# Weight forms split once, split tiles loaded three times, and a new order of the attention part, in a kernel of attention, linear memory and two MLPs

## The chip, the cores and the metric

The kernel runs on one core of one Trainium2 chip. The core has a matrix engine (TensorE, PE in the profile, with its weight load PEld beside it), VectorE (DVE), ScalarE (ACT), GpSimd (POOL) and a DMA queue that SyncE (SP) and ScalarE can issue to. Each engine runs its own list of instructions in order and waits on semaphores for the others. The metric is the device time of one execution in microseconds (us), the median over runs.

## The reference

q, k and v have 4 batches, 8 heads, 576 tokens and 64 columns. Each head's output is a gated mix of causal softmax attention and of a linear memory that is given (`M_prev`, `z_prev`). The 2304 x 512 result goes through two MLPs in float32; the weights arrive in float64.

```python
scores = where(causal, -1e9, q @ k.T / sqrt(D))
local  = (softmax(scores)) @ v
mem    = (phi(q) @ M_prev) / (phi(q) . z_prev + 1e-6)      # phi = elu + 1
x = g * mem + (1 - g) * local                              # g = sigmoid(beta) per head
h = x @ w_in;  r = maximum(h, 0)                           # 2304 x 2048
y = (s * r * r + b) @ w_out                                # 2304 x 512, s and b scalars
gate = sigmoid(y @ w_gate);  val = y @ w_val               # 2304 x 1536 each
out = (gate * val) @ w_out2                                # 2304 x 512
```

## The kernel before

Nearly every product is made of float32 values split in a high part (a cast to the PE's rounded format, written fp32r) and a low part (the value less its high part): high by high, low by high, high by low, three matmuls for one. The split is a cast on ACT and a subtraction on DVE or POOL.

The stages follow each other on PE. Attention runs in jobs of two heads: q and k come as raw tokens, are transposed on PE (`qt`, `kt`, L443), split, multiplied to scores (`sc`), put through the exponential, transposed (`pt`) and multiplied with v (`o`); the memory's products are `ret`. The jobs in `DIRECT` are written by `prep_direct` (its tiles at L964 to L1031), the others by `plan_prep`. Finished windows of x feed `h` (L321), whose rectified blocks go to DRAM (`relu_scratch`) and come back in `y`.

In `y` a step is one window of 384 tokens by 128 rows of r. `plan_step` loads it (`rr`, six buffers), squares it on ACT (L1446), makes s r^2 + b on POOL (`scale`, L1450), casts it (`gh`, L1456), subtracts (`gl` on DVE, L1461) and multiplies (L1475, 12 matmuls). After 16 steps `plan_y_out` brings the sums of a window out of PSUM (`evict`) and, but for the first two windows, stores them (`y_scratch`). During `y`, `plan_blocks` takes the float64 blocks of w_gate and w_val to float32 and makes seven forms of each group of weights (two copies and four sums and differences, `wm`), 12 groups, stored as plain float32 in `weight_scratch`.

The third stage takes the windows in three pairs. `plan_t` makes seven combinations of the two windows' y, split. `plan_group` (12 groups in a pair) loads a group's forms (`wf`, L1683, 896 KB), splits them (cast L1688 on ACT, subtraction L1696, one of four on DVE and three on POOL by `LOS`), multiplies the seven forms with the seven combinations (`m`, L1712, 42 matmuls), and adds the results up (`plus`, L1724 on DVE; sigmoid L1728 on ACT; the product of gate and value, `times`, L1734 on POOL). `plan_out` splits these products (`ps`, L1792 and L1805) and multiplies them with w_out2 (`o`, L1815, 216 matmuls in a pair). In the first pair the 12 tiles of w_out2 are brought from float64 too: three steps on DVE (L255, L258, L264), a cast (L270) and a subtraction on POOL (L273), in `weight_parts`.

What sets the order is a planner, the class `Plan`: every task is added with its engine, a cost in ns, an urgency made from the table `TUNE`, what it reads and writes, and which numbered buffers (`slots`) it takes. `order` plays the tasks against these costs and writes each engine's list. `RING` is the number of split tiles `ws`, `PACE` says after which steps of `y` a group's forms may be made.

Of the kernel before, what the change touches and what calls it, by code (L numbers as in the profile page):

```python
# [20 lines left out]
FB = 1  # L21
# [10 lines left out]
}  # L32
ENG = {"split": "DVE", "join": "POOL"}
# [4 lines left out]
RING = 5  # L38
SETS = 3
PACE = 2, 7  # L40


class Plan:
# [6 lines left out]
    def add(self, eng, ns, fn, urgency, reads=(), writes=(), new=(), late=60, size=0):  # L50
# [15 lines left out]
        self.tasks.append([eng, ns, fn, urgency, after, used, new, late, size])  # L66
        return n

    def order(self):
# [23 lines left out]
        out, events, now, dma = [], [], 0, 0  # L93
# [10 lines left out]
        while len(out) < len(tasks):  # L104
            for eng in clock:
                if clock[eng] > now:
                    continue
                for n in ready.get(eng, []):
# [44 lines left out]
def attention_moe_kernel(  # L153
# [41 lines left out]
    wf_d = dram("weight_scratch", [NF2, P, 7 * 2 * P])  # L195
# [15 lines left out]
    sb_b = const.tile([P, 1], F32, name="sb_b")  # L211

# [260 lines left out]
    def mm(n):  # L473
        return max(108, 15 + n // 2.35)
# [1481 lines left out]
```

## Time and profile before

| What | Value |
|---|---|
| median of 3 runs | 1077.78 us (1076.87 to 1078.69) |
| the profiled execution | 1078.23 us |
| its span in the trace | 1076.4 us |
| PE busy | 1043.2 us, 97% of the span, 6696 matmuls |
| DVE, ACT, POOL busy | 69%, 58%, 52% |
| DMA | 145.56 MB, mean 135 GB/s |

The span is the stretch between the first and the last instruction recorded; busy time is the sum over an engine's instructions with overlaps counted once. By the chain of waits (the work that ended last, followed back from the end) `h`, `m`, `y` and `o` of the third stage are the largest pieces. In the order of time the attention part fills about the first 80 us, then attention and `h` run mixed to about 400, `y` reaches to 646, the first pair to 797, the second to 935.

### The profile page before, as it was taken

Reading aid. Unit: us, or ns where it says so; the run is one execution under the profiler, and the core shown is the slowest. Engines: PE = TensorE matmul, PEld = TensorE weight load, DVE = VectorE, ACT = ScalarE, POOL = GpSimd, SP = SyncE. Lnnn points to the kernel's source line nnn. Section 1 sums busy time; section 2 is a strip of 40 time slices with the busy share of each in tenths; the row PEclk is TensorE's granted clock in tenths of the full one; section 3 lists DMA queues with packets and bytes.
Section 4 is the critical chain, followed back from the end, with each engine's and each line's share of the span. In section 5 each row is a group of like instructions: output and inputs, shape, how many; then the busy total and the mean of one; then the engine's idle time right before and its main releaser. Section 6 shows DMA issues by size and latency. Waiting matters only on the chain.

```text
span 1076.4 us, 19037 instructions
## 1 busy us (share of the span) xinstructions
PE 1043.2 (97%) x6696; PEld 981.2 (91%) x6696; DVE 741.1 (69%) x1408; ACT 623.8 (58%) x1341; POOL 560.9 (52%) x546
## 2 busy tenths in 40 slices
PE   6998999999999999999999999998999999999998
PEld 5887998899999999999999999887889998899986
DVE  4777887766776647557988747999736676266631
ACT  4766878767777656556667646554335453354431
POOL 1336466354344417535966537987428773277600
PEclk9998999999999999999999999999999999999999
DMA  5434453233332148657499766543223430133101
GB/s 136 108 78 124 141 162 102 73 100 92 88 88 69 50 142 271 205 180 251 149 332 299 258 246 219 182 162 108 88 79 123 138 104 30 64 137 109 63 20 40
DMA packets 135023, 145.56 MB, mean 135 GB/s; under 512 B 68112, under 2 KB 122896, under 8 KB 134928
## 3 DMA queue, kind: packets, MB, share of 16 engines
q1 hardware_dynamic: 134496, 144.35, 42.2%
q8 instruction: 53, 0.87, 0.3%
q14 instruction: 42, 0.34, 0.1%
q10 hardware_dynamic: 432, 0.01, 0.0%
HBM read 106.57 MB, written 37.75 MB: 134 GB/s over the span
## 4 chain that ended last, share of the span: by engine, by line
PE 82%; DVE 8%; POOL 4%; ACT 2%; DMA 2%; issue 2%; SPq 0%; DVEq 0%; ACTq 0%; POOLq 0%
PE h L321 18%; PE m L1712 18%; PE y L1475 17%; PE o L1815 14%; PE sc L673 3%; DVE set L1724 2%; PE o L1212 2%; PE acc L854 1%; PE acc L853 1%; PE pt_B L800 1%; DVE raw_w_out L258 1%; POOL rr L1450 1%; PE kt L443 1%; PE acc L857 1%; PE sc L699 1%
## 5 line engine op out<-in xcount | busy, mean ns | idle before, releaser
L1712 PE MATMUL m<-yt,ws 128*128 128x384 f32 x1512 | 265.2, 335 | 3.7 <-DVE set L1724 3.2
L1712 PEld LDWEIGHTS m<-yt,ws 128*128 128x128 f32 x1512 | 261.9, 188 | 6.8 <-DVE set L1724 4.9
L321 PE MATMUL h<-x,w_in 128*128 128x256 f32 (+1 forms) x1536 | 228.9, 301 | 1.9 <-DVE x L942 1.6
L321 PEld LDWEIGHTS h<-x,w_in 128*128 128x128 f32 x1536 | 210.0, 190 | 8.3 <-issue 3.2
L1724 DVE TENSOR_TENSOR set<-m,set 128x384 f32<-128x384 f32 x252 | 134.5, 554 | 58.7 <-PE m L1712 55.4
L1696 POOL TENSOR_TENSOR ws<-wf,ws 128x512 fp32r<-128x512 f32 (+1 forms) x108 | 124.3, 1171 | 83.5 <-ACT ws L1688 83.5
L1450 POOL TENSOR_SCALAR rr<-rr,sb_s,sb_b 128x384 f32<-128x384 f32 x96 | 111.6, 1170 | 99.6 <-ACT rr L1446 87.0
L1815 PE MATMUL o<-w_out,ps 128*128 128x512 f32 x648 | 154.5, 400 | 4.4 <-DVE ps L1805 4.2
L1815 PEld LDWEIGHTS o<-w_out,ps 128*128 128x128 f32 x648 | 123.5, 191 | 34.7 <-DVE ps L1805 4.5
L1475 PE MATMUL y<-gh,w_out 128*128 128x384 f32 x768 | 149.3, 335 | 1.1 <-POOL w_out L273 0.6
L1475 PEld LDWEIGHTS y<-gh,w_out 128*128 128x128 f32 x768 | 133.9, 188 | 2.1 <-POOL w_out L273 0.9
L1688 ACT CAST ws<-wf 128x512 fp32r<-128x512 f32 (+1 forms) x144 | 81.0, 567 | 88.1 <-PE m L1712 63.1
L1461 DVE TENSOR_TENSOR gl<-rr,gh 128x384 fp32r<-128x384 f32 x96 | 69.4, 728 | 56.8 <-ACT gh L1456 31.9
L1734 POOL TENSOR_TENSOR p<-set,set 128x384 f32<-128x384 f32 x72 | 84.1, 1188 | 43.1 <-DVE set L1724 43.1
L731 POOL TENSOR_SCALAR P<-P,rs 128x256 f32<-128x256 f32 (+4 forms) x108 | 62.7, 601 | 67.2 <-DVE rs L727 26.3
L653 DVE CUSTOM_DVE_ANT_0 P<-sc,mask 128x256 f32<-128x256 f32 (+4 forms) x144 | 69.9, 515 | 35.8 <-PE sc L673 13.8
L331 ACT ACTIVATE r<-h 128x320 f32<-128x320 f32 (+1 forms) x128 | 52.2, 409 | 72.6 <-PE h L321 58.5
L1475 PE MATMUL y<-gl,w_out 128*128 128x384 f32 x384 | 82.3, 335 | 0.8 <-DVE gl L1461 0.8
L1805 DVE TENSOR_TENSOR ps<-p,ps 128x512 fp32r<-128x512 f32 x54 | 49.4, 933 | 42.6 <-ACT ps L1792 42.3
L1792 ACT CAST ps<-p 128x512 fp32r<-128x512 f32 x54 | 32.5, 619 | 72.2 <-PE o L1815 60.6
L1475 PEld LDWEIGHTS y<-gl,w_out 128*128 128x128 f32 x384 | 67.8, 188 | 1.5 <-DVE gl L1461 1.5
L715 ACT ACTIVATE P<-P,nm 128x256 f32<-128x256 f32 (+4 forms) x108 | 62.9, 583 | 5.2 <-DVE nm L653 4.9
(185 smaller groups left out, 1623.8 us busy)
## 6 DMA issues: line engine op xcount, KB each, us to landing
wf<-weight_scratch SPq DMA_DIRECT2D x36, 896.0 KB, 4.6
rr<-relu_scratch SPq DMA_DIRECT2D x96, 192.0 KB, 4.0
raw_w_out<-in_moe_w_out_dram SPq DMA_DIRECT2D x28, 512.0 KB, 4.1
weight_scratch<-wm SPq DMA_DIRECT2D x12, 896.0 KB, 6.3
relu_scratch<-r SPq DMA_DIRECT2D x32, 320.0 KB, 2.4
raw_w_in<-in_moe_w_in_dram SPq DMA_DIRECT2D x16, 512.0 KB, 4.0
relu_scratch<-r SPq DMA_DIRECT2D x32, 256.0 KB, 2.8
raw_gv<-in_moe_w_gate_dram SPq DMA_DIRECT2D x12, 512.0 KB, 4.3
```

Of the source, the lines that this page charges most:

```text
L321: nc.tensor.matmul(t[:, :n], wt[:, wi, c], x[:, xi, c], start=(m == 0), stop=(m == 3 * NK - 1))
L653: nc.vector.tensor_tensor_reduce(out=pr, in0=ps, in1=mk, scale=1.0, scalar=3e38, op0=ALU.add, op1=ALU.min, accum_out=nm,)
L715: nc.scalar.activation(pr, pr, AF.Exp, bias=T.pop(("nm", j, e, t)), scale=-1.0, accum_out=T["sums", j][:, col : col + 1],)
L1450: nc.gpsimd.tensor_scalar(out=r, in0=r, scalar1=sb_s, scalar2=sb_b, op0=ALU.mult, op1=ALU.add)
L1461: nc.vector.tensor_tensor(out=gl, in0=r_sb.pop(step), in1=gs[step][0].bitcast(F32), op=ALU.subtract)
L1475: nc.tensor.matmul(accs[wi][d][:, :n], w_out_sb[f][:, x, d], y, start=(f == 0 and x == 0 and y is gh), stop=(f == NF - 1 and y is gl),)
L1688: nc.scalar.copy(t[:, 0, :m], flat(a, m))
L1696: engine[LOS[i]].tensor_tensor(out=t[:, 1, :m], in0=flat(a, m), in1=t[:, 0, :m].bitcast(F32), op=ALU.subtract)
L1712: nc.tensor.matmul(acc, wt[:, a, k : k + P], yt[:, y, c], start=(m == 0), stop=(m == 3 * K2 - 1),)
L1724: nc.vector.tensor_tensor(out=t[:, o], in0=Z["m", z, x], in1=t[:, i], op=ALU.add)
L1734: engine[TIMES[o]].tensor_tensor(out=p[:, f + HF * OF[o][0], OF[o][1]], in0=Z["set", z][:, o], in1=Z["set", zg][:, o], op=ALU.mult,)
L1815: nc.tensor.matmul(Z["zo", z], Z["ps", z, i][:, a, k * P : (k + 1) * P], w_out2_sb[f][:, x].rearrange("p c f -> p (c f)"), start=(i == k = ...
```

## The change

The matmuls of `h`, `y`, `m` and `o` stay as many as they were. Four things change.

*Forms.* `plan_blocks` splits each group's forms at once, as it makes them: `sums` makes the four sums and differences, `form` finds each pair of forms, `hi` casts it on ACT, `lo` subtracts on DVE (all four of `LOS`), `store` writes high and low part side by side. `weight_scratch` grows to four tiles of 128 x 1024 a group (the last half full). `plan_group` splits nothing; it loads the four tiles straight into `ws`, 4 loads where 1 was. `RING` goes from 5 to 7, `PACE` from (2, 7) to (0, 6).

*y.* `scale` goes; only r^2 is made. Two columns of ones beside the r of the first window give the column sums of w_out in the same matmuls (386 columns wide there, not 384), and s and b come in as y leaves PSUM.

*Pairs.* `SEQ` takes the pairs in the order 0, 2, 1: the last two windows of `y` go into the second pair as they are, so their stores and loads fall away (8 stores, 2 loads).

*Attention.* q and k have two raw buffers each, not one. The first q comes over ScalarE's queue. The memory's result (`MX`) sits in buffers of another tile. All costs of the planner and the table `TUNE` are new, and a task can hold a port that others wait for in the planner's play (`held`).

```diff
-RING = 5
+RING = 7
-PACE = 2, 7
+PACE = 0, 6
+LOS = ("DVE", "DVE", "DVE", "DVE")
-    "mem": 39.5, "lq": -622.0, "lk": -752.9, "lv": -921.7, "lm": 533.7, "q": -351.0,
+    "mem": -121814.8, "lq": 2020.0, "lk": -111329.7, "lv": 2438.5, "lm": 740.6, "q": -34627.0,
...
-    wf_d = dram("weight_scratch", [NF2, P, 7 * 2 * P])
+    wf_d = dram("weight_scratch", [NF2, 4, P, 1024])
...
-    rawq = at.tile([P, NQ, P], F32, name="rawq", bufs=1)
-    rawk = at.tile([P, NQ, P], F32, name="rawk", bufs=1)
+    rawqs = [at.tile([P, NQ, P], F32, name=f"rawq{i}", bufs=1) for i in range(2)]
+    rawks = [at.tile([P, NQ, P], F32, name=f"rawk{i}", bufs=1) for i in range(2)]
...
+        eng = nc.scalar if src is q and j == 0 else nc.sync
         for e in range(2):
-            nc.sync.dma_start(
+            eng.dma_start(
...
+    SEQ = [0, NW // 2 - 1, *range(1, NW // 2 - 1)]
...
+        def ones():
+            nc.gpsimd.memset(r_sb[step][:, n:], 1.0)
...
-        def scale():
-            r = r_sb[step]
-            nc.gpsimd.tensor_scalar(
-                out=r, in0=r, scalar1=sb_s, scalar2=sb_b, op0=ALU.mult, op1=ALU.add
-            )
...
+            if wi == 0:
+                nc.vector.tensor_scalar(
+                    out=sb_c[:, d : d + 1], in0=accs[wi][d][:, n : n + 1], scalar1=sb_b, scalar2=None,
+                    op0=ALU.mult,
+                )
...
-                nc.vector.tensor_copy(yf[wi][:, d], accs[wi][d][:, :n])
+                nc.vector.tensor_scalar(
+                    out=yf[wi][:, d], in0=accs[wi][d][:, :n], scalar1=sb_s,
+                    scalar2=sb_c[:, d : d + 1], op0=ALU.mult, op1=ALU.add,
+                )
...
-            if wi >= 2:
+            if wi // 2 not in (SEQ[0], SEQ[1]):
...
+        def hi(i):
+            box[i] = Y["ws"].tile([P, 2, 512], F32R, tag="ws", name=f"wp{n}_{i}")
+            nc.scalar.copy(half(i, 0), form(i)[0])
+
+        def lo(i):
+            engine[LOS[i]].tensor_tensor(
+                out=half(i, 1), in0=form(i)[0], in1=half(i, 0).bitcast(F32), op=ALU.subtract
+            )
+
+        def store(i):
+            m = form(i)[1] * P
+            nc.sync.dma_start(
+                wf_d[n, i, :, : 2 * m].rearrange("p (x m) -> p x m", x=2),
+                box.pop(i)[:, :, :m].bitcast(F32),
+            )
...
-        def load():
-            t = Z["wf", z] = Y["wf"].tile([P, 7, K2, P], F32, tag="wf", name=f"wf{pi}_{n}")
-            nc.sync.dma_start(t.rearrange("p a c f -> p (a c f)"), wf_d[n])
...
+        def load(i):
+            m = len(PAIRS[i]) * 2 * P
             t = Z["ws", z, i] = Y["ws"].tile([P, 2, 512], F32R, tag="ws", name=f"ws{pi}_{n}_{i}")
-            nc.scalar.copy(t[:, 0, :m], flat(a, m))
...
+            nc.sync.dma_start(
+                t[:, :, :m].bitcast(F32), wf_d[n, i, :, : 2 * m].rearrange("p (x m) -> p x m", x=2)
+            )
```

In the first pair POOL's list reads, before, at about the fourth group (`w_out_4` to `w_out_7` are tiles of w_out2, `ws` are low parts of forms, `p` products of gate and value):

```order
L273 TENSOR_TENSOR w_out_4_9015<-raw_w_out_4_9013,w_out_4_9015 128x512
L1696 TENSOR_TENSOR ws_3_3_9166<-wf_3_9027,ws_3_3_9166 128x256
L1734 TENSOR_TENSOR p_8852<-set_8_9108,set_2_9023 128x384 x3
L1696 TENSOR_TENSOR ws_9_1_9219<-wf_9_9111,ws_9_1_9219 128x512
L1696 TENSOR_TENSOR ws_9_2_9229<-wf_9_9111,ws_9_2_9229 128x512
L1734 TENSOR_TENSOR p_8852<-set_8_9108,set_2_9023 128x384
L1696 TENSOR_TENSOR ws_9_3_9254<-wf_9_9111,ws_9_3_9254 128x256
L273 TENSOR_TENSOR w_out_5_9127<-raw_w_out_5_9125,w_out_5_9127 128x512
```

After, at the same place:

```order
L278 TENSOR_TENSOR w_out_3_8921<-raw_w_out_3_8919,w_out_3_8921 128x512
L1809 TENSOR_TENSOR p_8893<-set_7_9013,set_1_8915 128x384 x4
L278 TENSOR_TENSOR w_out_4_9000<-raw_w_out_4_8998,w_out_4_9000 128x512
L278 TENSOR_TENSOR w_out_5_9057<-raw_w_out_5_9055,w_out_5_9057 128x512
L1809 TENSOR_TENSOR p_8893<-set_8_9164,set_2_9081 128x384 x4
L278 TENSOR_TENSOR w_out_6_9142<-raw_w_out_6_9140,w_out_6_9142 128x512
```

The low parts of forms are gone from it; products and tiles of w_out2 follow each other.

SP's list of loads at that place, before (`raw_w_out_7` is a tile of w_out2 in float64):

```order
L1683 DMA wf_4_9196<-weight_scratch 128x1792
L1683 DMA wf_10_9283<-weight_scratch 128x1792
L239 DMA raw_w_out_7_9294<-in_moe_w_out_dram 128x1024
L1683 DMA wf_5_9365<-weight_scratch 128x1792
L239 DMA raw_w_out_8_9379<-in_moe_w_out_dram 128x1024
```

and after:

```order
L1771 DMA ws_3_0_9113<-weight_scratch 128x1024
L1771 DMA ws_3_1_9135<-weight_scratch 128x1024
L244 DMA raw_w_out_6_9140<-in_moe_w_out_dram 128x1024
L1771 DMA ws_3_2_9152<-weight_scratch 128x1024
L1771 DMA ws_3_3_9186<-weight_scratch 128x2x256
L1771 DMA ws_9_0_9196<-weight_scratch 128x1024
L244 DMA raw_w_out_7_9200<-in_moe_w_out_dram 128x1024
```

One load of 1792 columns has become four, three of 1024 and one of 2 x 256.

At the start of the program ACT's list, with what each instruction waits for, is before:

```order
L215 DMA gt<-in_beta_dram 128x8
L216 DMA sb_s<-in_moe_s_dram 128x1
L217 DMA sb_b<-in_moe_b_dram 128x1
L218 ACT_TABLE_LOAD
L218 ACTIVATE gt<-gt 128x8 [waits DMAHW0_49]
L998 CAST KT_159<-kt_153 128x576 [waits PE_49]
L964 ACTIVATE phi_171<-qt_165 128x640 [waits PE_49]
L966 ACTIVATE QT_173<-qt_165 128x640
```

and after:

```order
L220 DMA gt<-in_beta_dram 128x8
L221 DMA sb_s<-in_moe_s_dram 128x1
L222 DMA sb_b<-in_moe_b_dram 128x1
L395 DMA rawq_91<-in_q_dram 128x4x64
L223 ACT_TABLE_LOAD
L223 ACTIVATE gt<-gt 128x8 [waits DMAHW0_49]
L395 DMA rawq_91<-in_q_dram 128x4x64 [waits DMAHW2_49]
L401 DMA rawq_91<-in_q_dram 64x64 [waits DMAHW4_49]
L401 DMA rawq_91<-in_q_dram 64x64 [waits DMAHW6_49]
L1002 ACTIVATE phi_174<-qt_165 128x640 [waits PE_49]
L1004 ACTIVATE QT_176<-qt_165 128x640
```

Four loads of q stand on ACT's queue now; DMAHW2, 4 and 6 are the semaphores of the loads of sb_s, of sb_b and of the third load of k. PE's list at the start is before:

```order
L443 MATMUL kt_153<-ident,rawk 128x128 x5
L443 MATMUL qt_165<-ident,rawq 128x128 x5
L1079 MATMUL sc_0_0_185<-KT_159,QT_173 128x128
L1079 MATMUL sc_1_0_186<-KT_159,QT_173 128x128
L1079 MATMUL sc_0_0_185<-KT_159,QT_173 128x128
```

and after:

```order
L451 MATMUL qt_165<-ident,rawq_91 128x128 x5
L1063 MATMUL ret_0_190<-mem_150,phi_174 128x65
L1063 MATMUL ret_1_191<-mem_150,phi_174 128x65
L1063 MATMUL ret_0_190<-mem_150,phi_174 128x65
L1063 MATMUL ret_1_191<-mem_150,phi_174 128x65
L1063 MATMUL ret_0_190<-mem_150,phi_174 128x65
L1063 MATMUL ret_1_191<-mem_150,phi_174 128x65
L1063 MATMUL ret_0_190<-mem_150,phi_174 128x65
L1063 MATMUL ret_1_191<-mem_150,phi_174 128x65
L1069 MATMUL ret_0_190<-mem_150,phi_174 64x65 x2
L451 MATMUL kt_206<-ident,rawk_93 128x128 x5
L451 MATMUL kt_229<-ident,rawk_94 128x128 x5
L1118 MATMUL sc_0_0_235<-KT_221,QT_176 128x128
```

The transposes of k stood first and come behind those of q and behind the ten matmuls `ret` now, those of the next job (`rawk_94`) right after, and the first scores behind both. Up to the first `h` PE's list has 425 rows before and 473 after.

## Rows read from the trace of the kernel before

**Rows 1.** The page, busy time, share of the span and instructions of each engine.

```profile
PE 1043.2 (97%) x6696; PEld 981.2 (91%) x6696; DVE 741.1 (69%) x1408; ACT 623.8 (58%) x1341; POOL 560.9 (52%) x546
```

**Rows 2.** Chain of waits, 645 to 935 us: start us, length us, what.

```profile
645.89 11.48 PE m L1712 x66
...
797.21 87.39 PE m L1712 x504
884.60 50.39 PE o L1815 x216
```

**Rows 3.** Windows: length, PE, PEld, DVE, ACT, POOL busy, clock, DMA share, GB/s.

```profile
0.00:80.00 80.00, 67.58 (x579) 57.52 (x580) 54.36 (x167) 50.10 (x96) 21.13 (x39) 0.98 0.44 107
80.00:400.00 320.00, 313.14 (x2502) 297.25 (x2501) 231.18 (x564) 231.87 (x576) 149.82 (x189) 0.99 0.35 100
400.00:550.00 150.00, 147.83 (x909) 145.57 (x908) 110.15 (x160) 93.01 (x197) 95.53 (x74) 1.00 0.69 224
475.00:650.00 175.00, 173.87 (x1000) 172.85 (x1000) 130.51 (x218) 106.24 (x224) 102.36 (x81) 1.00 0.75 249
675.00:750.00 75.00, 67.38 (x366) 63.07 (x364) 72.71 (x98) 41.63 (x80) 67.93 (x54) 0.99 0.46 155
800.00:875.00 75.00, 75.00 (x435) 75.00 (x434) 49.69 (x82) 38.69 (x73) 55.07 (x51) 1.00 0.37 124
```

**Rows 4.** Groups of lines, 646 to 746 us: busy us, mean ns | idle before.

```profile
L1724 DVE TENSOR_TENSOR set<-m,set 128x384 f32<-128x384 f32 x84 | 43.3, 551 | 6.1 <-PE m L1712 3.4 <-ACT f_w_out L252 0.7
L1696 POOL TENSOR_TENSOR ws<-wf,ws 128x512 fp32r<-128x512 f32 (+1 forms) x33 | 42.0, 1291 | 18.1 <-ACT ws L1688 18.1
L1734 POOL TENSOR_TENSOR p<-set,set 128x384 f32<-128x384 f32 x23 | 28.4, 1251 | 2.3 <-DVE set L1724 2.3
...
L258 DVE SCALAR_TENSOR_TENSOR raw_w_out<-raw_w_out 128x512 int32<-128x512 int32 x11 | 16.1, 1459 | 0.4
L273 POOL TENSOR_TENSOR w_out<-raw_w_out,w_out 128x512 fp32r<-128x512 f32 x10 | 13.8, 1378 | 4.0 <-ACT w_out L270 4.0
L264 DVE SCALAR_TENSOR_TENSOR raw_w_out<-f_w_out,raw_w_out 128x512 int32<-128x512 int32 x11 | 13.7, 1245 | 0.4
...
L1696 DVE TENSOR_TENSOR ws<-wf,ws 128x512 fp32r<-128x512 f32 x10 | 11.0, 1097 | 1.1 <-ACT ws L1688 0.9
L255 DVE TENSOR_SCALAR raw_w_out<-raw_w_out 128x512 int32<-128x512 int32 x11 | 9.8, 894 | 0.0
```

**Rows 5.** The same view for DVE, 900 to 925 us.

```profile
L1805 DVE TENSOR_TENSOR ps<-p,ps 128x512 fp32r<-128x512 f32 x10 | 6.8, 689 | 11.2 <-ACT ps L1792 11.2
```

**Rows 6.** The page, DMA issues: count, KB each, median us to landing.

```profile
wf<-weight_scratch SPq DMA_DIRECT2D x36, 896.0 KB, 4.6
rr<-relu_scratch SPq DMA_DIRECT2D x96, 192.0 KB, 4.0
...
rawq<-in_q_dram SPq DMA_DIRECT2D x32, 128.0 KB, 2.6
```

**Rows 7.** The page, GB/s in 40 equal slices of the span.

```profile
GB/s 136 108 78 124 141 162 102 73 100 92 88 88 69 50 142 271 205 180 251 149 332 299 258 246 219 182 162 108 88 79 123 138 104 30 64 137 109 63 20 40
```

**Rows 8.** The page, the costliest groups: the scale and shift in y.

```profile
L1450 POOL TENSOR_SCALAR rr<-rr,sb_s,sb_b 128x384 f32<-128x384 f32 x96 | 111.6, 1170 | 99.6 <-ACT rr L1446 87.0 <-DMA rr<-relu_scratch 6.5 <-DVE wm L1580 4.1
```

**Rows 9.** Chain of waits of the first 60 us: start us, length us, what.

```profile
1.24 4.78 DMA rawk<-in_k_dram
...
8.16 0.77 DVE KT L1002
...
8.97 1.34 PE qt L443 x5
...
11.67 0.84 DVE QT L974
...
12.55 2.40 PE sc L1079 x16
...
23.55 1.04 PE ret L1025 x16
```

More of the change, by code (lines that the diff above doesn't have):

```diff
@@ L65, in add @@
         used = set(reads) | set(writes) | {x for _, x in new}
-        self.tasks.append([eng, ns, fn, urgency, after, used, new, late, size])
+        self.tasks.append([eng, ns, fn, urgency, after, used, new, late, size, port])
         return n
@@ L742, in plan_scores @@
                 add(
-                    "PE", sum(3 * mm(keys(t)) for t in ts) + 190, lambda ts=ts: score(ts), w,
+                    "PE", sum(3 * mm(keys(t)) for t in ts) + 60, lambda ts=ts: score(ts), w,
                     reads=[("QT", j), ("KT", j)],
-                    new=[("s", ("sc", j, 0, ts[0])), ("s", ("sc", j, 1, ts[0]))], late=250,
+                    new=[("s", ("sc", j, 0, ts[0])), ("s", ("sc", j, 1, ts[0]))]
+                    + [(f"P{t}", ("P", j, e, t)) for e in range(2) for t in ts]
+                    + ([] if m else [("sums", ("sums", j))]),
+                    late=250,
                 )
@@ L1488, in plan_step @@
         )
-        add("ACT", act(n), square, v, writes=[rk])
-        add("POOL", 700, scale, v, writes=[rk])
-        add("ACT", act(n), g_hi, v, reads=[rk], new=[("gh", gk)])
-        add("DVE", 650, g_lo, v, reads=[rk, gk], new=[("gl", ("gl", step))])
+        if wi == 0:
+            add("POOL", 120, ones, v, writes=[rk])
+        add("ACT", act2(n), square, v, writes=[rk])
+        add("ACT", act2(n), g_hi, v, reads=[rk], new=[("gh", gk)])
+        add(
+            "DVE", **port(dve2(n)), fn=g_lo, urgency=v, reads=[rk, gk], new=[("gl", ("gl", step))]
+        )
         new = [("yacc", ("ya", wi))] if f == 0 else []
@@ new lines, in lo @@
+        def lo(i):
+            engine[LOS[i]].tensor_tensor(
+                out=half(i, 1), in0=form(i)[0], in1=half(i, 0).bitcast(F32), op=ALU.subtract
+            )
+        def store(i):
[3 more added lines that the diff above has]
+                box.pop(i)[:, :, :m].bitcast(F32),
+            )
+        k0, k1 = (("raw", x) for x in keys2)
+        for part in range(2):
+            add(
+                "DVE", **port(850), fn=lambda part=part: sums(part), urgency=u,
+                reads=[k0, k1, "bar2"], writes=[("wm", n)] if part else [],
+                new=[] if part else [("wf", ("wm", n))],
+            )
@@ new lines, in plan_blocks @@
+        for i, xs in enumerate(PAIRS):
+            m, k = len(xs) * 2 * P, ("wp", n, i)
+            ins = [k0, "bar2"] if i == 0 else [k1, "bar2"] if i == 3 else [("wm", n)]
+            add("ACT", act2(m), lambda i=i: hi(i), u, reads=ins, new=[("ws", k)])
+            add(
+                LOS[i], **port((dve2 if LOS[i] == "DVE" else pool2)(m)), fn=lambda i=i: lo(i),
+                urgency=u, reads=ins, writes=[k],
+            )
+            add(
+                "SP", 450, lambda i=i: store(i), u, reads=[k], writes=[("wd", n, i)], late=2500,
+                size=m * 1024,
+            )
```

282 lines of the change are left out of this document (149 added, 133 removed), and 12 rows, old and new, of the table TUNE.

## The prediction

> **What bounds the kernel now.** I read the page first: TensorE (PE) is busy 1043.2 of 1076.4 us, 97% [rows 1]. So the kernel is a queue of matmuls, and a change that leaves their number alone, as this one does, can win only what PE waits. The chain of waits gives the pace of a stage that nothing holds up: in the second pair of token windows 504 `m` matmuls took 87.39 us (173.4 ns each) and 216 `o` matmuls 50.39 us [rows 2], together 137.8. The first pair ran from 645.89 to 797.21, so 151.3 us for the same work: 13.5 us lost [rows 2]. The windows show why and where else [rows 3]: from 675 to 750 POOL is busy 67.9 of 75 us and VectorE (DVE) 72.7, and PE idles 7.6; from 800 to 875, where nothing is lost, DVE has 49.7 and POOL 55.1. In attention PE idles 12.4 us up to 80 and 6.9 from 80 to 400. From 400 to 550 it idles 2.2. All that is 13.5 + 12.4 + 6.9 + 2.2 = 35.0 us, some 3% of the time; PE's idle time counts only whole gaps, and the 67.6 busy us up to 80 hold many short matmuls that overlap, so attention has somewhat more to give than its 19.3.
>
> The profiled execution took 1078.23 us, its span 1076.4, 1.8 lie around it; it is 0.45 above the median of 1077.78. The sum is made against 1078.2.
>
> **Part 1: forms split once.** Each of three pairs now loads the weight forms as high and low parts. Before, each group split them on chip: in the first pair POOL did 33 such subtractions in the window shown at 1291 ns, 42.0 us, and DVE 10 at 1097 ns [rows 4]. All of that goes from `m`. What stays for POOL in the first pair: 24 products at 1251 ns and 12 low parts of w_out2 at 1378 ns, 30.0 + 16.5 = 46.6 us of 87.4. What stays for DVE: 84 sums at 551 ns = 46.3, and 12 tiles of w_out2 at 1459 + 1245 + 894 = 3.60 us = 43.2; together 89.5, still over 87.4. But those three durations are those of a crowded stretch. A subtraction of 128x512 took 1097 ns there, and 689 ns at 900 to 925, in the second pair's `o` stretch [rows 4, 5], where POOL has no products left to make. At 689/1097 the w_out2 tiles cost 27.1 us and DVE's sum is 73.4. So DVE lands between 73 and 90 of 87 us, and I take it nearer to the lower end, since POOL goes from full to about half: 4 of the 13.5 us stay, **9.5 are won**. The ends: all 13.5 (DVE at the quiet price), or a loss, which only the transfers can make (below).
>
> The row that carries this is the pair of durations, 1097 and 689. The Trainium skill (SBUF — State Buffer, Who interferes with whom) says that VectorE and GpSimd share one pair of ports as an exclusive lock, and that a VectorE operation with two SBUF inputs waits for all of a GpSimd operation that reads SBUF. The trace agrees in kind; by that rule each of the 36 products and low parts that POOL keeps can still hold a DVE instruction for its whole length, and DVE would end nearer 90 than 73, with a gain of 3 or 4 instead of 9.5. That is the third rival.
>
> **The transfers that this adds.** A group's load grows from 896 KB [rows 6] to twice that, three tiles of 128x1024 words and one of 128x512, 1.835 MB. In a pair that is 12 x 1.835 = 22.0 MB in 87.4 us, 252 GB/s where 124 stand now [rows 3]. The whole kernel's best slice moved 332 GB/s [rows 7], so pairs two and three stay covered with a quarter to spare: cost 0. If the cover went and the queue gave only the 249 GB/s of 475 to 650 [rows 3], a pair would take 88.4 us, 1 more each. In the first pair the 12 tiles of w_out2 come on top, each 128x1024 words, 6.3 MB: 28.3 MB in 87.4 us is 324 GB/s. At 332 that takes 85 us and is just hidden; at 249 it takes 113.7, against 100.9 now, 12.8 worse than before. I keep it within the 4 us that I left there.
>
> In `y` the stores of the forms double, 12 x 0.918 = 11.0 MB more, and 8 stores of y go, each 128x384 words, 1.6 MB. Between 475 and 650 the queue moved 249 GB/s at a share of 0.75 [rows 3], 43.6 MB; now 53.0 MB, 303 GB/s and a share of 0.91. At the three best neighbouring slices (332, 299, 258, mean 296 [rows 7]) that takes 179 us, 4 over the 175; at 332 it takes 160 and costs nothing; at 249 it would be 38 over. Behind a late load of relu(h) stand square, cast and subtraction, all in order, and PE after them; a step is 12 matmuls at the pace of `m`, 2.08 us, and six buffers cover 12.5 us against a landing of 4.0 [rows 6]. **I take 3 us lost**, between the first two ends, since the loads of weights can wait and the covered 12.5 us is far over 4.0.
>
> **Part 2: r^2 alone in y.** 96 POOL instructions of 1170 ns go, 111.6 us of POOL [rows 8], against 16 tiny fills and 4 one-column products. Most of that lies beside a busy PE. It pays where POOL was last: the idle time of 400 to 550, **2.2 us** won (ends: 0 and 2.2). DVE gets new work in `y`: per block three subtractions of 128x512 and one of half that, 3.5 x 0.689 = 2.4, so 12 x 2.4 = 29 us [rows 5], where 130.5 of 175 us are used now [rows 3]; 160 of 175 is tight but fits, and POOL's 102.4 us there shrink by most of the 96 x 1.17, which shortens DVE's own. Cost 0; if it did not shorten them, the blocks would end late and `m` start up to 5 us late.
>
> **Part 3: last tokens stay on chip; order of pairs 0, 2, 1.** Two loads and eight stores go, all hidden now; no matmul moves against its neighbours. Cost 0, ends 0 and -1.
>
> **Part 4: attention: two raw buffers and a new order.** Here the start is worse than it looks. The first four loads of q go from SP to ScalarE's queue, but the rows of the order show the last three waiting for semaphores of earlier transfers, the last of them for k's third load, which lands at 6.0 [rows 9]. A landing of 2.6 us [rows 6] after that, and q is whole at 8.6 at the earliest; its transposes start at 8.97 now [rows 9], so nothing is gained there. From then to a split q takes 3.5 us (8.97 to 12.51), so 12.1. PE's order then puts the ten memory products `ret` ahead of k's transposes: they need one more DVE pass, as long as the 0.84 of q's, and take 10/16 of 1.04: 13.6. From a whole k to a split one 2.9 us pass (6.02 to 8.93), so the first scores start at about 16.5 against 12.55 [rows 9], 4 us later. Of these a part comes back: `ret` and the next job's k are done by then, work that came later before, and DVE, which does it, is the fullest helper up to 80 with 54.4 us [rows 3]. After the start the second raw buffers let SP load a job ahead, and the order was made anew; the trace of before cannot price that. From both sides: half of the 19.3 idle us won, -9.7, or the 4 us kept whole and as much again lost to a first `h` that now stands behind 473 and not 425 other rows of PE, +8. I take the middle of the lower half: **4 us won**, since twice as many buffers give most of the idle time a way out, and the late start is paid once.
>
> **Sum.** 1078.2 - 9.5 + 3.0 - 2.2 - 4.0 = 1065.5; less 0.45 for the median: **1065 us**.
>
> **The rivals.**
> 1. *Slower: the DMA queue becomes the bound of `y` and of the first pair.* Place: 475 to 740. For it: a share of 0.91 and 324 GB/s; the 224 GB/s of 400 to 550, at 0.69, already stand beside 2.2 idle us [rows 3]. Against it: 332 GB/s was reached beside a PE that lost nothing. It decides when the queue sustains less than about 285 GB/s: at 270, `y` takes 196 us (+21), the first pair 105 (+4), and with attention's -4 and the -2.2 the time is 1078 + 19 = 1097. At 290, +8 and -3 leave 1077.
> 2. *Attention gives nothing or loses.* For it: the late q and the later `h`; attention at +8 instead of -4: 1077. Against it: the next job's k is ready earlier.
> 3. *The first pair stays tight* (DVE at the crowded price): 3.5 won instead of 9.5: 1071. For it: 89.5 of 87.4 us. Against it: POOL's share halves.
> 4. *Attention wins more:* prefetch and order take away 15 us, since the 12.4 + 6.9 idle us and the short matmuls around them both give: 1054.
> 5. *The change does not do what it says:* loads of the split forms that come late in every pair, 1 us each: 1067, inside the forecast.
>
> **How the numbers follow.** Forecast with its own range 1058 to 1071 (rivals 3 and 5 are its upper part): 0.60. Rival 4, 1044 to 1057: 0.16. Rival 2, 1072 to 1080: 0.13. Rival 1, above 1080 with the part at 1077: 0.11. A measurement of this kernel tells about 0.2%, 2.2 us: faster means below 1075.6. Faster: 0.60 + 0.16 + 0.08 of rivals 1 and 2 = 0.84. Same: 0.07. Slower: 0.09. The range of 8 in 10 leaves out a part of rival 4 below 1049 and of rival 1 above 1080.
>
> **What would show it.** First pair: the `m` and `o` stretch of 151.3 us at about 142, POOL and DVE below 9 tenths. `y`: DMA share near 0.9 from 475 to 650, and few waits on `rr`. Pairs two and three still 137.8 with 250 GB/s. First scores near 16.5 us, first `h` at 80 or later. The forecast is wrong if waits on `ws` or `rr` loads stand before PE, or if PE's idle time up to 400 differs from 15 by more than 8.

## The result, and the profile after

The changed kernel takes 1064.9 us (median of 4 runs, 1064.64 to 1066.66) against 1077.3 for the kernel before beside it (1076.62 to 1078.69): the ratio is 0.9885, interval 0.9869 to 0.9901. The forecast was 1065 us. The sum came out; four of its terms did not, and their errors cancel.

The profiled execution took 1065.1 us, its span 1063.0. The page's first part, as in [rows 1]:

```profile
PE 1037.5 (98%) x6696; PEld 979.9 (92%) x6696; DVE 696.1 (65%) x1424; ACT 564.4 (53%) x1221; POOL 315.0 (30%) x361
```

POOL lost 246 us of work and DVE 45. The chain of waits, where [rows 2] stood (start us, length us, what):

```profile
645.18 81.14 PE m L1787 x468
...
783.81 87.37 PE m L1787 x504
871.18 50.40 PE o L1884 x216
```

The first pair starts where it did (645.2 against 645.9) and ends at 783.8 instead of 797.2: 138.6 us, not 151.3. The second pair takes 137.8 as before. The windows of [rows 3] (length, PE, PEld, DVE, ACT, POOL busy, clock, DMA share, GB/s):

```profile
0.00:80.00 80.00, 63.31 (x563) 54.38 (x564) 57.11 (x173) 50.42 (x98) 23.16 (x45) 1.00 0.54 131
80.00:400.00 320.00, 316.13 (x2521) 298.42 (x2521) 226.18 (x558) 231.65 (x576) 146.67 (x187) 0.99 0.33 94
400.00:550.00 150.00, 149.47 (x917) 148.81 (x917) 118.66 (x192) 104.93 (x214) 32.55 (x35) 1.00 0.76 261
475.00:650.00 175.00, 174.35 (x994) 173.77 (x993) 139.03 (x258) 119.61 (x238) 10.69 (x5) 1.00 0.86 302
675.00:750.00 75.00, 74.42 (x405) 70.88 (x404) 59.27 (x96) 32.85 (x59) 38.03 (x31) 1.00 0.63 217
800.00:875.00 75.00, 75.00 (x429) 74.24 (x428) 43.74 (x76) 20.54 (x39) 23.62 (x23) 1.00 0.66 209
```

From 675 to 750 PE idles 0.6 us where it idled 7.6, with DVE at 59 of 75 and POOL at 38. Up to 80 it idles 16.7, more than the 12.4 of before, and from 80 to 400 3.9 instead of 6.9. By the starts of the stages in the two traces, the 13.4 us of the span divide so:

| stretch | before | after | won |
|---|---|---|---|
| start to first `y` matmul | 402.3 | 401.7 | 0.5 |
| first `y` to first `m` | 243.5 | 243.3 | 0.2 |
| first pair, `m` and `o` | 151.3 | 138.6 | 12.7 |
| the rest | 279.4 | 279.4 | 0.0 |

Nearly all of it is the first pair. Some of it is TensorE's granted clock, which the two kernels did not have alike. These are the windows 70 to 110 and 745 to 760 before, and 70 to 110 after; from 730 to 745, the like place of the first pair, the changed kernel has 1.00:

```profile
70.00:110.00 40.00, 36.57 (x278) 31.70 (x277) 31.61 (x79) 25.18 (x59) 20.87 (x23) 0.87 0.48 127
745.00:760.00 15.00, 10.61 (x35) 8.12 (x35) 12.65 (x14) 4.82 (x9) 8.04 (x5) 0.77 0.00 0
```

```profile
70.00:110.00 40.00, 36.70 (x312) 32.37 (x313) 32.01 (x88) 29.25 (x68) 19.88 (x23) 0.96 0.38 100
```

Of the two levels, 1.2 and 2.4 GHz, PE had the lower one for parts of these stretches. That lost 40 x 0.13 = 5.2 and 15 x 0.23 = 3.4 us before, and 40 x 0.04 = 1.6 after. So some 3.4 of the 12.7 us of the first pair were lost clock, at the end of `m`, where `o` had waited 4.2 us for `ps`. In attention 3.6 us less of clock were lost, and only 0.5 us were won.

The groups of lines of the first pair, 646 to 746 us, that answer to [rows 4]:

```profile
L1799 DVE TENSOR_TENSOR set<-m,set 128x384 f32<-128x384 f32 x84 | 44.5, 553 | 20.4 <-PE m L1787 12.8 <-ACT f_w_out L257 6.7
L1809 POOL TENSOR_TENSOR p<-set,set 128x384 f32<-128x384 f32 x24 | 25.5, 1072 | 4.4 <-DVE set L1799 4.2
L278 POOL TENSOR_TENSOR w_out<-raw_w_out,w_out 128x512 fp32r<-128x512 f32 x12 | 16.5, 1372 | 163.1 <-DVE set L1799 127.8 <-ACT w_out L275 35.2
...
L263 DVE SCALAR_TENSOR_TENSOR raw_w_out<-raw_w_out 128x512 int32<-128x512 int32 x12 | 9.3, 776 | 0.4
L269 DVE SCALAR_TENSOR_TENSOR raw_w_out<-f_w_out,raw_w_out 128x512 int32<-128x512 int32 x12 | 8.3, 694 | 1.2
...
L260 DVE TENSOR_SCALAR raw_w_out<-raw_w_out 128x512 int32<-128x512 int32 x12 | 5.2, 434 | 0.0
```

The sums `set` cost 553 ns as before; the steps on w_out2 fell from 1459, 1245 and 894 ns to 776, 694 and 434. DVE waits for PE now, which is the order of things one wants.

The start has become later. The chain of the first 30 us, as [rows 9]:

```profile
2.33 5.30 DMA rawq<-in_q_dram
...
9.21 1.32 PE qt L451 x5
...
13.49 1.97 PE ret L1063 x16
...
15.87 1.27 PE kt L451 x5
...
18.65 1.33 PE kt L451 x5
19.98 2.54 PE sc L1118 x12
```

The first scores start at 19.9 us. In the kernel before the first two started at 11.7 and the other 16, which [rows 9] shows, at 12.55, so they are 8 us later; the first `h` at 87.6 instead of 79.2. By the 1024th `h` matmul (358.3 and 358.2) the two kernels are level.

### The profile page after: what moved, and what is told of

The parts are those of the page before. It is cut to its first block, busy times and chain, and to the rows that moved or that the text cites. A ratio compares the mean times of both kernels' runs of the same rounds, so it can differ in the third digit from the quotient of the medians.

```text
span 1063.0 us, 18848 instructions
## 1 busy us (share of the span) xinstructions
PE 1037.5 (98%) x6696; PEld 979.9 (92%) x6696; DVE 696.1 (65%) x1424; ACT 564.4 (53%) x1221; POOL 315.0 (30%) x361
## 4 chain that ended last, share of the span: by engine, by line
PE 95%; ACT 2%; DVE 2%; issue 1%; DMA 1%; POOL 0%; ACTq 0%; DVEq 0%; POOLq 0%
PE m L1787 24%; PE h L326 19%; PE y L1519 18%; PE o L1884 14%; PE sc L704 3%; PE o L1251 2%; PE acc L888 2%; PE acc L889 2%; PE pt_B L835 1%; PE sc L730 1%; PE sc L1118 1%; PE kt L451 1%; PE qt L451 1%; PE acc L892 1%; PE pt_D L835 1%
## 5 line engine op out<-in xcount | busy, mean ns | idle before, releaser
L326 PE MATMUL h<-x,w_in 128*128 128x256 f32 (+1 forms) x1536 | 224.9, 300 | 0.0
L1519 PE MATMUL y<-gh,w_out 128*128 128x384 f32 (+1 forms) x768 | 150.7, 338 | 0.7 <-ACT r L336 0.5
L1809 POOL TENSOR_TENSOR p<-set,set 128x384 f32<-128x384 f32 x72 | 75.6, 1056 | 187.8 <-DVE set L1799 186.8
L278 POOL TENSOR_TENSOR w_out<-raw_w_out,w_out 128x512 fp32r<-128x512 f32 x28 | 37.8, 1350 | 214.3 <-DVE set L1799 127.8
L1795 ACT COPY set<-m 128x384 f32<-128x384 f32 x36 | 17.3, 481 | 111.5 <-PE m L1787 111.5
L762 POOL TENSOR_SCALAR P<-P,rs 128x384 f32<-128x384 f32 (+4 forms) x108 | 64.7, 621 | 30.4 <-DVE rs L758 18.8
L1504 DVE TENSOR_TENSOR gl<-rr,gh 128x384 fp32r<-128x384 f32 x96 | 57.7, 609 | 22.5 <-PE y L1519 12.5
L1874 DVE TENSOR_TENSOR ps<-p,ps 128x512 fp32r<-128x512 f32 x54 | 46.1, 883 | 35.8 <-ACT ps L1861 35.5
L746 ACT ACTIVATE P<-P,nm 128x384 f32<-128x384 f32 (+4 forms) x108 | 62.6, 581 | 10.1 <-DVE nm L684 9.8
L1803 ACT ACTIVATE set<-set 128x384 f32<-128x384 f32 x72 | 37.6, 524 | 57.1 <-DVE set L1799 57.1
```

What stands on the lines that cost most here:

```text
L326: nc.tensor.matmul(t[:, :n], wt[:, wi, c], x[:, xi, c], start=(m == 0), stop=(m == 3 * NK - 1))
L746: nc.scalar.activation(pr, pr, AF.Exp, bias=T.pop(("nm", j, e, t)), scale=-1.0, accum_out=T["sums", j][:, col : col + 1],)
L762: nc.gpsimd.tensor_scalar(out=pr, in0=pr, scalar1=T["rs", j, part][:, n : n + 1], scalar2=1.0, op0=ALU.mult, op1=ALU.mult,)
L1504: nc.vector.tensor_tensor(out=gl, in0=r_sb.pop(step)[:, :n], in1=gs[step][0][:, :n].bitcast(F32), op=ALU.subtract,)
L1519: nc.tensor.matmul(accs[wi][d][:, : y.shape[1]], w_out_sb[f][:, x, d], y, start=(f == 0 and x == 0 and y is gh), stop=(f == NF - 1 and y i ...
L1809: engine[TIMES[o]].tensor_tensor(out=p[:, f + HF * OF[o][0], OF[o][1]], in0=Z["set", z][:, o], in1=Z["set", zg][:, o], op=ALU.mult,)
```

## The experiments

All are edits of the changed kernel. Times are medians; the kernel before, beside them, had 1077.2 to 1078.5.

**What the first pair waited for.** Three kernels put removed work back on tiles that nothing reads, so that only the load of the engines returns and not the chain load, cast, subtraction, product. After a `product(x)` of the first pair:

```diff
+            if pi == 0 and r in POOL_FILL:            # {1: 512, 3: 512, 5: 256}
+                fill("POOL", POOL_FILL[r])            # t - t on a spare tile
+            if pi == 0 and r in DVE_FILL:             # {3: 480}
+                fill("DVE", DVE_FILL[r])
```

Both:

> The changed kernel with the work that was taken from the first pair put back without its chain: per group two subtractions of 128x512 and one of 128x256 on POOL and one of 128x480 on DVE, on spare tiles that nothing reads. Theory 1 (DVE was the bound of the first pair, made slow by POOL's work beside it): DVE's steps on w_out2 go back toward 0.9, 1.45 and 1.25 us, DVE is nearly full from 675 to 750, the first pair takes 148 to 152 us instead of 138.6, time 1074 to 1078. Theory 2 (the pair waited for the chain load, cast, subtraction of each tile, and the engines' load did not matter): no one waits for the added work, the pair stays under 141 us and the time under 1067.

POOL alone:

> The changed kernel with only POOL's share of the removed work put back in the first pair, two subtractions of 128x512 and one of 128x256 per group on a spare tile that nothing reads. With both shares put back the first pair took 151.5 us. Theory 1 (POOL's work makes DVE's instructions longer, and that alone fills DVE): DVE's w_out2 steps are long again (about 0.8, 1.2, 1.1 us), DVE needs 46 + 37 = 83 to 85 us of 87, and the pair takes 141 to 146 us, time 1068 to 1073. Theory 2 (DVE's own ten subtractions were what did not fit): the pair stays within 1 us of 138.6, time under 1066.5.

DVE alone:

> The changed kernel with only DVE's share of the removed work put back in the first pair: one subtraction of 128x480 per group on a spare tile. POOL's share alone made the pair 145.0 us, both shares 151.5, none 138.6. Theory 1 (DVE is the bound only while POOL's work makes its instructions long; then the shares do not add): DVE's added steps take some 0.65 us, 8 us in all, DVE stays under 70 of 75 us, the pair stays within 1.5 us of 138.6, time under 1066.5. Theory 2 (the shares add): the pair takes 144 to 146 us as both less POOL's, time 1070 to 1072.

Measured, the time and the length of the first pair in the profiled run:

| put back | time | ratio to before | first pair |
|---|---|---|---|
| nothing | 1064.9 | 0.9885 (0.9869 to 0.9901) | 138.6 |
| DVE's share | 1065.2 | 0.9883 (0.9857 to 0.9909) | 138.9 |
| POOL's share | 1071.4 | 0.9942 (0.9924 to 0.9960) | 145.0 |
| both | 1078.4 | 1.0006 (0.9994 to 1.0019) | 151.5 |

Both shares give the whole loss back, to 0.2 us, with no chain behind them. The windows 675 to 750 of DVE's share alone, POOL's alone, and both:

```profile
675.00:750.00 75.00, 74.16 (x404) 70.65 (x403) 63.93 (x104) 33.06 (x59) 38.98 (x30) 1.00 0.63 218
```

```profile
675.00:750.00 75.00, 69.70 (x380) 66.98 (x379) 68.58 (x95) 29.23 (x55) 67.44 (x57) 0.98 0.62 224
```

```profile
675.00:750.00 75.00, 68.66 (x376) 64.89 (x374) 71.82 (x103) 25.56 (x47) 62.55 (x54) 1.00 0.65 231
```

And one DVE step on w_out2 with DVE's share alone, then with POOL's alone:

```profile
L265 DVE SCALAR_TENSOR_TENSOR raw_w_out<-raw_w_out 128x512 int32<-128x512 int32 x12 | 9.3, 777 | 0.4
```

```profile
L265 DVE SCALAR_TENSOR_TENSOR raw_w_out<-raw_w_out 128x512 int32<-128x512 int32 x12 | 16.2, 1350 | 0.4
```

The same DVE instruction takes 777 ns beside a POOL that is half idle (776 in the changed kernel) and 1350 beside a full one. So POOL's low parts make DVE's work longer. How the loss reaches PE is not the same in all. In the kernel before and with both shares `m` waits for DVE's sums, 3.2 and 2.9 us. With POOL's share alone `m` does not wait at all: its first 468 matmuls take 81.31 us, as in the changed kernel. PE's longest wait of the pair before, and the one of POOL's share alone (total, times, longest):

```profile
PE o L1815 <- DVE ps L1805: 4.2, 1, 4.2
```

```profile
PE o L1901 <- ACT ps L1878: 5.0, 1, 5.0
```

The 5.0 us, 0.3 of a second wait and 1.7 of granted clock (0.89 from 738 to 753), less the 0.6 that the changed kernel waits there, are the whole 6.4. The chain that ends in this wait has two long steps of DVE, and then POOL's own list, two of the added subtractions among it, up to the products:

```profile
732.36 1.35 DVE raw_w_out L271
...
734.47 1.74 POOL w_out L280
736.21 1.00 POOL sparePOOL L1801
737.21 1.81 POOL yf L1708
739.02 0.57 POOL sparePOOL L1801
739.59 2.29 POOL p L1826 x2
```

So here POOL's share costs PE by longer steps on DVE and by late products of POOL itself, and no run parts the two. DVE's share costs 0.3 us alone, and 6.5 once POOL is full. The theory of the chain load, cast, subtraction fell: the loss is back without it.

**The start.** Two kernels undo one part of the late start each. In the first the first q load is issued by SP again (`eng = nc.sync`), ahead of k's:

> The changed kernel with its first q load back on SP's queue, ahead of k's; all other lists unchanged. Theory 1 (attention won nothing because its start came 7 to 8 us late, and what comes after gave only that back): q's transposes start near 6.2 us instead of 9.2, the memory products near 11.7 instead of 13.5, the first scores near 18 instead of 19.9, and 1 to 3 us of that reach the end: 1062 to 1064 us. Theory 2 (the attention part is paced by the helper engines further on, and an early start is given back there): the first scores are earlier, the 1024th h matmul still starts near 358 us, time 1064.9 within 1 us.

In the second k's transposes of the first job, with cast and subtraction, are moved ahead of q's:

```diff
-        for n in plan.order():
+        seq = [n for n in plan.order() if n not in MOVE["k", 0]]
+        at_q = seq.index(MOVE["q", 0])
+        for n in seq[:at_q] + MOVE["k", 0] + seq[at_q:]:
```

> The changed kernel with k's transposes of the first job, their cast and subtraction moved ahead of q's transposes; the memory products still stand before the scores. Theory 1 (late start): k is split by 9 us as in the kernel before, the first scores start near 17.2 instead of 19.9, and 2 to 3 us reach the end: about 1062.5 us. Theory 2 (given back further on): first scores near 17.2, the 1024th h matmul near 358 us as now, time within 1 us of 1064.9.

q on SP gave 1061.9 us (0.9862, 0.9839 to 0.9884), k first 1061.9 (0.9855, 0.9837 to 0.9873). The first scores start at 16.7 and 17.1 us, and the gain is still there at the 1024th `h` (354.5 and 354.7) and at the end: spans of 1059.6 and 1060.0. Either edit alone makes the changed kernel 3 us faster (the intervals of the ratios still touch its own), so the start had eaten up most of attention's gain.

Then the first scores alone were moved to where they stood before, ahead of the memory products and the next job's k, by a list of the first 16 tasks:

```diff
+        head = [171, 172, 173, 166, 167, 168, 169, 170, 176, 185, 177, 179, 181, 183, 186, 188]
+        seq = plan.order()
+        at_q = seq.index(166)
+        for n in seq[:at_q] + head + seq[at_q:]:
+            if n not in done:
```

> The changed kernel with the first job's start in the order of the kernel before: k's transposes, q's, the first three tiles of scores with their maxima, then the memory products and the next job's k. Theory 1 (each us by which the first scores come earlier reaches the end, as k first gave 3.0 us for 2.8): first scores near 12.8 instead of 17.1, time 1057 to 1059. Theory 2 (that held for the first 3 us, beyond it the softmax work of DVE and ACT sets the pace): 1060 to 1062.

The scores start at 11.9, 8 us earlier than in the changed kernel, and next to nothing came of it: 1065.7 us (0.9894, 0.9869 to 0.9920), in the profiled run a span 0.7 shorter. Both theories fell. PE's matmuls from 18.5 us (start us, length us) in the changed kernel, with k first, and in this one show what had not moved:

```profile
22.45 1.33 PE L451 MATMUL qt<-ident,rawq 128*128 128x128 f32 x5
```

```profile
19.91 0.77 PE L451 MATMUL qt<-ident,rawq 128*128 128x128 f32 x5 [0.18 <-DVE KT L1042]
```

```profile
21.99 1.33 PE L451 MATMUL qt<-ident,rawq 128*128 128x128 f32 x5 [2.71 <-DVE KT L1040]
```

These are q's transposes of the second job. Where a row names a wait, it is for the subtraction `KT` of that job's k, which in the last kernel stood on DVE behind the memory's `MX` and three steps on w_in. Set against the changed kernel their start moved by 2.5, 0.5 and, with q on SP, 3.3 us, and the span by 3.0, 0.7 and 3.4.

A second thing moved with them. The five transposes take 1.33 us in the changed kernel and in the last one, and 0.77 with k first (and with q on SP): PE was at the lower level of its clock in the one case and at the higher in the other. In the traces the record of the higher level begins at 23.9 us in the changed kernel, 25.4 in the last, 19.6 with k first and 19.0 with q on SP (17.9 in the kernel before). What that is worth can be estimated from kernels below that have the changed kernel's list there and its transposes at 22.5: with rows of 400 words the record begins at 22.5 us and the first `h` at 87.1, with doubled stores at 24.2 and 87.6, so 0.3 us for each us. By this estimate 1.3 to 1.5 of the 3 us came with the clock.

A last order was to test the rule of the transposes, by a longer `head`: the second job's k ahead of the memory products, the exponentials of the first tiles, and the second job's q ahead of the steps on w_in.

> The changed kernel with both first jobs put first: k's transposes, q's, three tiles of scores, the next job's k ahead of the memory products, the exponentials and the next job's q ahead of the first steps on w_in. Putting the scores of the first job ahead alone moved them 8 us and the end by less than 1. Theory 3 (the time follows the start of the second job's q transposes, 22.5 us in the changed kernel with 0, 22.0 in the last order with -0.7, 19.9 with k first and -3.0, 19.1 with q on SP and -3.4): they start near 19 here, and the span falls by 3.3 to 3.8 us, time 1061 to 1061.7. Theory 4 (what counts is the softmax chain of the first job, whose exponentials run some 5 us earlier here): the span falls by 5 us or more, time under 1060. Theory 5 (later steps on w_in, put behind, take it back): time 1063 or more.

The transposes start at 18.6, but the time is 1073.0 us (0.9941, 0.9915 to 0.9968). The windows say why (16 to 24, 24 to 32, 32 to 40 and 40 to 48 us):

```profile
16.00:24.00 8.00, 7.98 (x43) 5.99 (x42) 5.51 (x14) 5.54 (x11) 0.00 (x0) 1.00 0.52 115
```

```profile
24.00:32.00 8.00, 6.30 (x43) 5.43 (x41) 6.62 (x17) 6.23 (x13) 1.30 (x1) 0.79 0.53 131
32.00:40.00 8.00, 7.26 (x45) 6.90 (x46) 3.00 (x13) 4.64 (x10) 2.04 (x2) 0.66 0.55 121
40.00:48.00 8.00, 8.00 (x39) 7.35 (x37) 4.00 (x9) 2.11 (x5) 0.14 (x1) 0.50 0.41 110
```

The granted clock falls to its lower level, 1.2 GHz, for most of 28 to 48 us: (0.21 + 0.34 + 0.50) x 8 = 8.4 us lost, about as much as the span grew (7.7). Five of its six runs had a mean clock of 0.987 to 0.989; the sixth, at 0.994, took 1066.6. So the rule about the second job's q fits the three orders from which it was read, with the earlier clock as a rival, and the fourth does not test it. What makes the clock rise and hold there is open.

**y: the POOL pass.** A pass times 1, plus 0 on POOL was put back between square and cast:

```diff
+            nc.gpsimd.tensor_scalar(
+                out=r, in0=r, scalar1=1.0, scalar2=0.0, op0=ALU.mult, op1=ALU.add
+            )
```

> The changed kernel with a POOL pass over r^2 put back between square and cast, in the place where scale and shift stood (times 1, plus 0): 96 passes of some 1.0 to 1.2 us. Theory 1 (POOL was last at the hole of y, and its work lengthened DVE's): PE waits again in y, from its last h to the first m 171 to 174 us instead of 169.5, time 1066.5 to 1069. Theory 2 (the hole came from the transfers or the order): within 1 us of 1064.9.

1082.1 us (1.0048, 1.0030 to 1.0067), far over both: from the first `y` to the first `m` 260.1 us instead of 243.3. ACT's waits from 475 to 660 us (total, times, longest):

```profile
ACT gh L1503 <- POOL rr L1497: 36.1, 43, 2.2
```

ACT's list in the changed kernel has a square and its own cast close together, since nothing stands between them; with POOL in between ACT stood still 36 us. In the kernel before the list has squares of other steps in between, and ACT waited 3.0 us for this pass from 475 to 645. DVE's `gl` took 638 ns against 608, so here it is the chain and not the neighbour. The experiment says what the pass would cost in this order; it does not give the price of the pass in the order before.

**y: the transfers.** Each store of the split forms made twice:

```diff
+            for d in (wf_d2, wf_d):
                 nc.sync.dma_start(
```

> The changed kernel with every store of the split forms made twice, the second to a buffer that nothing reads: 22 MB more in y, 75 MB in 475 to 650 us if nothing gives way, 429 GB/s, where the best slice so far moved 389. Theory 1 (the queue in y is near its bound, so the doubling of the forms was hidden only just): relu loads land late, PE waits in y, y ends 10 to 28 us later, time 1075 to 1093. Theory 2 (there is room, since weights can wait and relu loads are six deep): y ends less than 3 us later, time under 1068.

1092.9 us (1.0139, 1.0123 to 1.0155): 271.2 us from the first `y` to the first `m`, 27.9 more. The windows 475 to 550, 550 to 600 and 600 to 675, and ACT's wait for relu loads:

```profile
475.00:550.00 75.00, 68.05 (x382) 66.16 (x381) 59.18 (x102) 47.75 (x93) 10.62 (x5) 1.00 0.90 329
550.00:600.00 50.00, 48.01 (x270) 46.85 (x270) 36.60 (x72) 30.08 (x63) 0.00 (x0) 1.00 1.01 380
600.00:675.00 75.00, 63.08 (x330) 59.86 (x329) 43.38 (x83) 40.71 (x81) 0.00 (x0) 0.95 1.04 392
```

```profile
ACT rr L1496 <- DMA rr<-relu_scratch: 49.0, 26, 5.2
```

So the way in which the transfers would have lost is real: the queue is full at 380 to 392 GB/s and PE starves. In `y` the change asks 302 and stays below it. In its first pair it asks for more, 335 GB/s at a share of 0.97 from 660 to 720, and PE is busy all of the 60 us.

**y: where rows begin.** The tiles `rr` and `gh` grew from 384 to 386 words for the two columns of ones. Two kernels changed only this width, to 400 words for both, and to 512 for `gh` and 448 for `rr`:

```diff
-            r = Y["gp"].tile([P, WT + 2], F32, tag="r", name=f"rr{wi}_{f}", bufs=RR)
+            r = Y["gp"].tile([P, 448], F32, tag="r", name=f"rr{wi}_{f}", bufs=RR)
...
-            gh = Y["gp"].tile([P, WT + 2], F32R, tag="gh", name=f"gh{wi}_{f}", bufs=GG)[:, :wide]
+            gh = Y["gp"].tile([P, 512], F32R, tag="gh", name=f"gh{wi}_{f}", bufs=GG)[:, :wide]
```

> The changed kernel with the rows of the rr and gh tiles 400 words wide instead of 386 (the same columns are used). Theory 1: the y matmuls, which take 175.3 ns each where they took 173.4 before, are slowed by where the rows of 386 words begin; with 400 they take 173.4 again, 960 of them 166.5 us instead of 168.7, and the time falls by 2.0 to 2.4 us to about 1062.7. Theory 2: it is the heavier DMA traffic in y; then they stay at 175.3 ns and the time at 1064.9.

> The changed kernel with gh rows of 512 words and rr rows of 448, so that every gh and gl tile begins at a multiple of 512 bytes in its pool, as in the kernel before. With rows of 400 words y's matmuls took 174.4 ns, with 386 words 175.4, before 173.4. Theory 1 (where the operand's rows begin sets it): 173.3 to 173.5 ns, y 1.9 us shorter, time 1062.8 to 1063.5. Theory 2 (something else in y, as the heavier transfers): 174.4 or more, time 1064 to 1065.5.

The `y` matmuls with `gh` from 550 to 600 us (mean ns of one last but one) before, after, with 400 and with 512 words:

```profile
L1475 PE MATMUL y<-gh,w_out 128*128 128x384 f32 x193 | 37.5, 334 | 0.0
```

```profile
L1519 PE MATMUL y<-gh,w_out 128*128 128x384 f32 x192 | 37.6, 337 | 0.0
```

```profile
L1519 PE MATMUL y<-gh,w_out 128*128 128x384 f32 x193 | 37.7, 336 | 0.0
```

```profile
L1519 PE MATMUL y<-gh,w_out 128*128 128x384 f32 x194 | 37.6, 334 | 0.0
```

From start to start they take 173.4, 175.4, 174.4 and 173.4 ns. 400 words gave 1065.4 us (0.9886, 0.9867 to 0.9904), no gain that can be told; 512 gave 1063.3 (0.9867, 0.9841 to 0.9893), 1.6 less than the changed kernel, in intervals that overlap; `y` took 242.1 us in the trace against 243.3. The rate alone would make 1152 x 2 ns = 2.3, but the first window's matmuls, 386 columns wide, stayed at 177 ns. The first theory holds for the pace: these widths bring the pace of before back, under the same transfers. That the rows begin at multiples of 512 bytes is what 384 and 512 words have in common; whether less would do, no run shows.

**Both gains together**, k first and 512 words:

> The changed kernel with the two edits that gained alone: k's transposes of the first job ahead of q's (3.0 us), and gh rows of 512 words, rr rows of 448 (1.6 us, y's matmuls at 173.4 ns). Theory 1 (the two lie in different stages, attention and y, and add): 1060.3 us, within 0.6; the second job's q at 19.9 us, y's matmuls at 173.4 ns. Theory 2 (y's gain depends on where the clock falls earlier, since in the profiled run with 512 words it fell near 30 us): 1062 or more in most runs.

1062.0 us (five runs from 1059.62 to 1063.84; 0.9848, 0.9833 to 0.9863). That beats both kernels, but not k first alone (1061.9). The two runs with a mean clock of 0.998 took 1059.6 and 1060.0, what the sum says; the other three, at 0.994 to 0.996, 1062.0 to 1063.8, as the second theory had it. In the profiled one the clock is down early:

```profile
20.00:32.00 12.00, 10.69 (x62) 8.85 (x62) 7.86 (x26) 8.17 (x17) 1.21 (x1) 0.72 0.70 160
```

With k first alone the same stretch has 1.00. PE's list is the same in both up to there. The profiled runs with both shares put back and with 512 words lost clock there too (0.70 from 25 to 30 and 0.62 from 30 to 35 us), although their list there is that of the changed kernel, whose run did not. What decides is open.

## Why the prediction came out

**Part 1, forms: right in the main, too small in size.** 9.5 us were forecast and 12.7 won. The step that was mis-sized is the one that put DVE between the crowded and the quiet price and left 4 of the 13.5 us: the steps on w_out2 came at 434, 776 and 694 ns, 1.90 us a tile against 3.60, so DVE's sum is 46 + 23 = 69 us, below even the quiet end of 73. POOL at half its load was already quiet enough. The row it rested on, the pair 1097 and 689 in [rows 4, 5], was the right one: the fills show that POOL's load is what lengthens DVE's steps. Two things were not in the prediction: that some 3.4 of the 13.5 us were granted clock, which came back whole with the wait, and that a full POOL also brings its own products late.

By the rule of the Trainium skill (SBUF — State Buffer, Who interferes with whom), that a VectorE operation with two SBUF inputs contends with a GpSimd one that reads SBUF, DVE was to end near 90. The kind agrees (777 against 1350 ns), the size does not: 36 POOL instructions of 1.07 to 1.37 us stayed, and the DVE steps were still quiet. The rule says what can happen when the two meet, and how often they meet has to come from the trace. With the sum so far under 87 us the rival of a tight first pair fell.

**The transfers: no loss, 3 us forecast.** The load was right, 303 GB/s forecast and 302 measured, the share 0.91 and 0.86; PE waited 0.5 us in all of `y`. The step that failed took three neighbouring slices of [rows 7], a mean of 296 GB/s, for what the queue can give. Those slices were what was asked for; asked for more, it gave 380 to 392. In the first pair, where 324 were forecast, 335 were moved at no cost. Pair two moved 209 GB/s (252 forecast) at no cost, as forecast.

**Part 2: 2.2 forecast, 0.2 left.** The idle time from 400 to 550 fell from 2.2 to 0.5 us, as the term says. What was missed is a cost on PE itself, in none of the terms: two more columns in the tile made 1152 matmuls 2 ns longer each. It does not show as a wait; PE is busy all the time.

**Part 3: nothing**, as forecast.

**Part 4, attention: 4 us forecast, 0.5 won.** The late start was seen and undersized: the scores were to start at 16.5 and started at 19.9. q was whole by 9.2 rather than 8.6. The memory products took 2.4 us rather than 0.65: the ten rows of the list are 16 and 4 instructions in the trace, so 10/16 of 1.04 was too little, and PE was still at the lower level of its clock, as the same group later shows.

```profile
28.04 1.11 PE L1063 MATMUL ret<-mem,phi 64*128 64x65 f32 x16
```

In the chain of the first 30 us above they take 1.97 us. The second k, ahead of the scores in PE's list, had been left out. The step that failed is the last: that twice as many buffers give more than the late start costs. They gave as much, and 3.6 us less of lost clock is in that too. PE's idle time up to 400 us came to 20.6, within the 8 us about 15 that the prediction allowed itself. Undoing either half of the late start brings 3 us, and with that attention would have been near the 4 of the forecast.

The first pair gave 3.2 us more than forecast, `y` 1.0 more (0.2 won where 3.0 - 2.2 = 0.8 was to be lost), attention 3.5 less: 0.7 us in all, of errors of up to 3.5. The mechanism that carried the forecast, less POOL and so shorter steps on DVE, was right; that the sum came within a microsecond was luck.

## What to carry to other kernels

Before taking work off an engine that looks full, read the same instruction's duration beside a busy and beside an idle neighbour: here 36 POOL subtractions that nothing reads cost PE 6.4 us, by longer steps on DVE and by the products queued behind them. A list that is ordered anew is not judged by its first output: the scores came 8 us earlier for 0.7, and with k first 2.8 us earlier for 3.0. Read the granted clock beside every stage before its time is put down to an order: here 7 us less of lost clock stand beside 13.4 us won. A GB/s that a trace shows is a demand until something waits for it.

## What the runs showed of the hardware

With `gh` rows of 386 words in the pool `y`'s matmuls took 175.4 ns, with 400 words 174.4, with 512 words 173.4, the same 384 columns read; those of `gl` too, whose own rows stayed 384 wide but lie behind the others. DVE's 128x512 integer step on SBUF took 777 ns beside POOL at 39 of 75 us and 1350 beside POOL at 67, while its sums that read PSUM took 552 and 550. The same 16 `ret` matmuls took 1.97 us at 13.5 us of the changed kernel and 1.11 at 28.0. The DMA engines moved 392 GB/s over 75 us (600 to 675 of the kernel with the doubled stores), with PE waiting, and 335 over 60 us (660 to 720 of the changed kernel) with PE busy throughout.
